# Gated recurrence and gated feed-forward on one core: the first 512 tokens share tiles, banks and copies; weight loads are issued first; the last tile is done in two strips

## The chip, the cores and the metric

The kernel runs on one core of one Trainium2 chip. The metric is the device time of one execution in microseconds. Lower is better.

## The reference

Two layers follow each other over 23,296 tokens (4 sequences of 5,824) with 256 channels. The first is a gated linear recurrence; the second is a feed-forward layer whose two up projections are multiplied.

```python
sig_r, sig_i = sigmoid(r_gate), sigmoid(i_gate)
a_t  = exp(8.0 * sig_r * log(clip(sigmoid(a_param), 1e-6, 1 - 1e-6)))
norm = sqrt(maximum(1 - a_t * a_t, 1e-6))
h[t] = a_t[t] * h[t-1] + norm[t] * sig_i[t] * x[t]       # per channel, h = 0 at the start of each sequence
out  = ((h @ w1) * (h @ w2)) @ w3 @ w_out                # 256 -> 1024, 1024 -> 1024, 1024 -> 256
```

## The kernel before

The tokens are cut into 47 chunks: `sizes = [256, 256] + [512] * 44 + [256]`. Chunks 0 and 1 share the gate stage (they are loaded and gated as one block of 512), but have scans, casts, up products and down products of their own. Channels lie on the 128 partitions in two blocks (`cb`), time along the free axis.

A chunk goes through these steps; the letters are those of the order string, and numbers behind them are the chunk and then a half, channel block or pair:

- `r`, `i`, `x` load the three inputs (SyncE's DMA queue, `load`, L142). `R` and `I` take tanh of half the gate on ScalarE (L150, L162); `p` adds 1 to the second and `t` multiplies it by x (GpSimd, or VectorE where the sets say so; L168, L172).
- `V` and `U` turn both from time-major to channel-major, through TensorE and a PSUM tile for the first chunks (L191), or by a transposing DMA.
- `d` is the exponential that gives a_t (ScalarE, L212), `s` its square, `q` the square root (ScalarE; this and tanh need different tables, and each switch shows as an ACT_TABLE_LOAD), `g` the gated input (VectorE, L237), `h` the scan (VectorE, L251), `y` the cast of the scan's result to bf16 (L268).
- `a` and `b` are the up products with w1 and w2 on TensorE (L286 to L299): 8 blocks of 128 hidden units, in 4 pairs `mp`, each over 2 channel blocks. `c` copies an `a` product from PSUM to SBUF (L307, ScalarE or VectorE), `m` multiplies the copy with the `b` product of the pair (VectorE, L313).
- `D` are the down products of one tile of 128 tokens (8 matmuls that accumulate, L323), `e` copies the sum out of PSUM (L335, L340), `o` stores it.

The product w3 @ w_out is computed once on the chip, into `wp_sb`: `Lw3`, `Cw3` load and cast a block of w3, `Ft` turns it on TensorE, `Fc` copies it out, `Fm` multiplies it with w_out, `Fe` copies the result out with a factor 0.25. `Lw1`, `Lw2`, `Lwo` and `Cw1`, `Cw2`, `Cwo` load and cast the other weights in halves; their fp32 staging tiles are slots of the rings `a` and `nrm`. `A0` to `A3` compute the recurrence's rates from a_param. `W` are groups of two warm-up matmuls on an identity, with no use of the result.

There is no loop over chunks: `ORDER`, a string of some 2,450 steps, says in which order the steps are given out, and each engine runs its own in that order. An instruction that waits holds up all that stand behind it on its engine; DMA issues stand in SyncE's order. Sets such as `DV_COPY`, `AC_SQUARE`, `W_ACT`, `FOLD_ACT` say which engine a step runs on. Tiles come from rings (`RINGS`): PSUM has a ring `po` of 4 banks, for `a` products, down products, turned tiles and the fold, and a ring `pb` of 2 pairs of banks, for `b` products and warm-ups. A step that takes a slot waits until the last user of that slot is done.

The order begins like this:

```python
r0 i0 x0 A3. E A0. A1. A2. R0.1 R0.0 W7 W10 V0.1 V0.0 W3 W14 W4 d0.1 s0.1 d0.0 s0.0 I0 q0.0 t0.0 t0.1 U0 g0
h0.0 W1 W2 W12 W5 W13 W8 W0 W15 h0.1 q0.1 g1 h1.1 h1.0 Lw1.0 Cw1.0 y0.1 y0.0 i2 Lw2.0 I2 r2 Lw1.1 Cw2.0 a0.0.1
a0.0.0 a0.1.0 a0.1.1 b0.0 R2 Cw1.1 x2 y1.1 y1.0 p2 t2.0 Lw3.2 Cw3.2 Lw2.1 Lwo.1 t2.1 c0.0.1 c0.1.1 c0.0.0
```

Of the kernel before, what the change touches and what calls it, by code (L numbers as in the profile page):

```python
# [18 lines left out]
LOG1P = (2.00000001, 0.66666316, 0.40024854, 0.27961419, 0.28174657)  # L19
# [3 lines left out]
def kernel(  # L23
# [59 lines left out]
    DV_PLUS = {16}  # L83
    DV_HALF = set()
    DV_SQUARE = {(0, 1), (11, 0)}
    AC_SQUARE = {(2, 0), (2, 1), (3, 0), (3, 1), (4, 0), (4, 1), (5, 0), (7, 0), (8, 0), (10, 0), (11, 1), (12, 0),
        (14, 0), (14, 1), (15, 0), (15, 1)}
    DV_CAST = set()
    AC_CAST = set()
    DV_COPY = {(0, 0, 0), (0, 0, 1), (0, 1, 0), (0, 1, 1), (0, 2, 0), (1, 0, 0), (1, 0, 1), (1, 1, 0), (1, 1, 1), (1,  # L90
        3, 0), (2, 0, 1), (2, 1, 0), (2, 1, 1), (2, 2, 0), (2, 3, 0), (2, 3, 1), (3, 0, 0), (3, 1, 0), (3, 2, 1), (3,
        3, 0), (4, 0, 0), (4, 0, 1), (4, 1, 1), (4, 2, 0), (4, 2, 1), (5, 1, 1), (5, 3, 0), (5, 3, 1), (6, 0, 0), (6,
        0, 1), (6, 2, 0), (6, 3, 1), (7, 0, 0), (7, 2, 0), (7, 3, 0), (7, 3, 1), (8, 3, 0), (10, 0, 1), (10, 1, 0),
        (10, 1, 1)}
    DV_EVAC = {(2, 0), (8, 0), (8, 1), (9, 0), (9, 1)}
    FOLD_ACT = {('c', 7), ('e', 3), ('e', 4)}
    W_ACT = {('w1', 1), ('w2', 0), ('w3', 0)}
    W_DVE = set()
# [3 lines left out]
    WARM = [2] * 16  # L102
    RINGS = {"r": 4, "i": 5, "x": 4, "th_r": 3, "u": 2, "rt": 2, "ut": 6, "a": 6, "nrm": 6, "h": 2, "y": 4,
# [38 lines left out]
    def load(c, nm):  # L142
        n = width(c) // P
        t = ring(loads, [P, 4, D], F32, name=nm + "_t", tag=nm)
        nc.sync.dma_start(
            out=t[:, :n, :],
            in_=src[nm][starts[c]:starts[c] + width(c), :].rearrange("(p n) c -> p n c" if long_rows(c) else "(n p) c -> p n c", p=P))
        T[nm, c] = t
# [102 lines left out]
    def scan(c, cb):  # L251
        w = sizes[c]
        first = ("h", c) not in T
        if first:
            T["h", c] = ring(ypool, [P, NCB, CT], F32, name="h_t", tag="h")
        h = T["h", c][:, :, :w]
        a, n = (T[key, gates_of(c)][:, :, part(c)] for key in "an")
        if first:
            for b in range(1, B):
                if 0 < b * S - starts[c] < w:  # L260
                    nc.vector.memset(a[:, :, b * S - starts[c]:b * S - starts[c] + 1], 0.0)
        init = 0.0
        if starts[c] % S != 0:
            pw = sizes[c - 1]
            init = T["h", c - 1][:, cb, pw - 1:pw]
        nc.vector.tensor_tensor_scan(h[:, cb, :], a[:, cb, :], n[:, cb, :], init, ALU.mult, ALU.add)  # L266

    def cast(c, cb=None):  # L268
        w = sizes[c]
        if ("y", c) not in T:  # L270
            T["y", c] = ring(ypool, [P, NCB, CT], BF16, name="y_t", tag="y")
        key = c if cb is None else (c, cb)
        cbs = slice(None) if cb is None else cb
        y, h = T["y", c][:, cbs, :w], T["h", c][:, cbs, :w]
# [11 lines left out]
    def up(c, m, dst, w_sb):  # L286
        w = sizes[c]
        for cb in range(NCB):
            nc.tensor.matmul(out=dst[:, :w], lhsT=w_sb[:, cb, m * P:(m + 1) * P],  # L289
                             rhs=T["y", c][:, cb, :w], start=(cb == 0), stop=(cb == NCB - 1))  # L290

    def up_a(c, mp, q):
        T["pa", c, mp, q] = pp = ring(psum_o, [P, CT], F32, name="pa", tag="po")
        up(c, 2 * mp + q, pp, w1_sb)

    def up_b(c, mp):
        T["pb", c, mp] = pp = ring(psum_b, [P, 2, CT], F32, name="pb", tag="pb")
        for q in range(2):
            up(c, 2 * mp + q, pp[:, q, :], w2_sb)  # L299
# [7 lines left out]
    def copy(c, mp, q):  # L307
        w = sizes[c]
        if ("sa", c, mp) not in T:
            T["sa", c, mp] = ring(ffn, [P, 2, CT], BF16, name="sa", tag="sa")  # L310
        copy_to((c, mp, q) in DV_COPY, T["sa", c, mp][:, q, :w], T["pa", c, mp, q][:, :w])

    def product(c, mp):  # L313
        w = sizes[c]
        if ("g", c) not in T:
            T["g", c] = ring(ffn, [P, KD, CT], BF16, name="g_t", tag="g")
        nc.vector.tensor_mul(out=T["g", c][:, 2 * mp:2 * mp + 2, :w], in0=T["sa", c, mp][:, :, :w],  # L317
                             in1=T["pb", c, mp][:, :, :w])

    def pair(c, j2):  # L320
        return min(2, sizes[c] // P - 2 * j2)

    def down(c, j):  # L323
        if c == NCH - 1:
            T["po_last", j] = po = ring(psum_o, [P, D], F32, name="po", tag="po")
        else:
            if ("po", c, j // 2) not in T:
                T["po", c, j // 2] = ring(psum_o, [P, 2, D], F32, name="po", tag="po")
            po = T["po", c, j // 2][:, j % 2, :]
        for k in range(KD):  # L330
            nc.tensor.matmul(out=po,  # L331
                             lhsT=T["g", c][:, k, j * P:(j + 1) * P], rhs=wp_sb[:, k, :],
                             start=(k == 0), stop=(k == KD - 1), skip_group_check=True)
# [6 lines left out]
    def evac_last(c, j):  # L340
        if ("ot", c, j // 2) not in T:
            T["ot", c, j // 2] = ring(ffn, [P, 2, D], F32, name="ot", tag="ot")
        copy_to(j % 2 == 0, T["ot", c, j // 2][:, j % 2, :], T["po_last", j])

    def store_last(c, j):
        t0 = starts[c] + j * P
        nc.sync.dma_start(out=out[t0:t0 + P, :], in_=T["ot", c, j // 2][:, j % 2, :])
# [41 lines left out]
    def fold_t(mi):  # L389
# [244 lines left out]
```

## Time and profile before

| | |
|---|---|
| median of 3 runs | 511.69 us (511.57 to 511.84) |
| the profiled execution | 511.82 us, of which 510.0 us lie between its first and last instruction (the span) |
| busy in the span | TensorE 502.2 us, ScalarE 463.3, VectorE 429.8, GpSimd 318.2 |
| granted TensorE clock | 1.00 in every stage |
| DMA | 124.06 MB, mean 243 GB/s; 387 to 419 GB/s in most stretches of the first 30 us |
| first up product, first down products | 13.30 us, about 47.9 us |

A row of the profile's timeline gives the start in us, the duration in us, the engine, the line, the operation, the tiles written and read, the shape of the operands and the count of merged instructions; in brackets stands how long the engine was idle before it, and what released it. In this table and in the profile, PE is TensorE, PEld its weight loads, DVE VectorE, ACT ScalarE, POOL GpSimd and SPq the instruction queue of SyncE, which issues the DMAs. A busy TensorE can still be one that runs warm-up work, and matmuls overlap, so a sum of durations is more than their time; the distance from start to start is the better measure.

### The profile page before, as it was taken

The numbers are of one execution on the slowest core, as the hardware profiler recorded it, in microseconds if no ns is written. First come the engines' busy times: TensorE is split into PE (matmuls) and PEld (weight loads), VectorE is DVE, ScalarE is ACT, GpSimd is POOL, SyncE is SP. The second block draws the span as 40 slices with busy tenths as digits, with TensorE's granted clock in tenths as the row PEclk, the third lists the DMA queues.
The fourth block names the chain that finished last, engine by engine and source line by source line (L and its number), as shares of the span: only waits on it lengthen the run. The fifth ranks groups of instructions, "written<-read, shape, count | busy, mean of one in ns | idle before, by whom it ended". The sixth has DMA issues, their size and how long they took to land.

```text
span 510.0 us, 8879 instructions
## 1 busy us (share of the span) xinstructions
PE 502.2 (98%) x3217; PEld 308.2 (60%) x3217; DVE 429.8 (84%) x417; ACT 463.3 (91%) x711; POOL 318.2 (62%) x274
## 2 busy tenths in 40 slices
PE   7999999999999999999999999999999999999997
PEld 3777655665565656556666556565566655656566
DVE  5999999999999789878879799878877797959762
ACT  7999999998999999999999999998998979888543
POOL 3775878557558936965786973956647568580200
PEclk9999999999999999999999999999999999999999
DMA  8999999999989997896999996898786895252313
GB/s 319 407 413 307 379 275 276 304 302 257 309 232 282 303 282 248 191 322 184 256 306 317 262 285 163 233 245 227 206 250 151 231 319 149 91 164 64 66 48 105
DMA packets 177904, 124.06 MB, mean 243 GB/s; under 512 B 87362, under 2 KB 173892, under 8 KB 177860
## 3 DMA queue, kind: packets, MB, share of 16 engines
q1 hardware_dynamic: 177856, 123.50, 85.2%
q8 instruction: 25, 0.41, 0.3%
q14 instruction: 19, 0.16, 0.1%
q10 hardware_dynamic: 4, 0.00, 0.0%
HBM read 78.91 MB, written 23.86 MB: 201 GB/s over the span
## 4 chain that ended last, share of the span: by engine, by line
PE 90%; ACT 4%; DVE 2%; issue 2%; DMA 1%; DVEq 0%; ACTq 0%
PE po L331 30%; PE pb L289 29%; PE pa L289 28%; PE pw L403 1%; ACT sa L305 1%; PE ptr L197 1%; DVE g_t L317 1%; DMA r_t<-in_r_gate_dram 1%; PE ptw L392 1%; DVE sa L303 1%; DVE h_t L266 1%; ACT L165 1%; ACT L235 1%; ACT nrm L235 0%; ACT i_t L165 0%
## 5 line engine op out<-in xcount | busy, mean ns | idle before, releaser
L317 DVE TENSOR_TENSOR g_t<-sa,pb 128x1024 bf16<-128x1024 bf16 (+1 forms) x188 | 218.6, 1180 | 60.6 <-PE pb L289 29.0
L289 PEld LDWEIGHTS <-w_sb 128*128 128x128 bf16 x1504 | 146.5, 98 | 144.0 <-issue 3.4
L305 ACT CAST sa<-pa 128x512 bf16<-128x512 f32 (+1 forms) x336 | 180.9, 588 | 27.7 <-PE pa L289 17.6
L289 PE MATMUL pa<-y_t,w_sb 128*128 128x512 bf16 (+1 forms) x752 | 190.6, 372 | 0.4 <-ACT sa L305 0.2
L289 PE MATMUL pb<-y_t,w_sb 128*128 128x512 bf16 (+1 forms) x752 | 185.2, 372 | 0.6 <-DVE g_t L317 0.6
L331 PE MATMUL po<-wp_sb,g_t 128*128 128x256 bf16 x1456 | 178.0, 273 | 0.0
L331 PEld LDWEIGHTS <-g_t 128*128 128x128 bf16 x1456 | 142.4, 98 | 40.6 <-issue 0.5
L278 POOL CAST y_t<-h_t 128x1024 bf16<-128x1024 f32 (+2 forms) x49 | 52.5, 1074 | 146.0 <-DVE h_t L266 142.2
L189 POOL TENSOR_TENSOR u_t<-i_t,x_t 128x512 bf16<-128x512 f32 (+1 forms) x90 | 122.2, 1374 | 4.1 <-issue 2.0
L266 DVE TENSOR_TENSOR_SCAN h_t<-a_t,h_t,nrm 128x512 f32<-128x512 f32 (+1 forms) x92 | 120.8, 1343 | 1.6
L230 POOL TENSOR_TENSOR nrm<-a_t 128x512 f32<-128x512 f32 x74 | 83.0, 1139 | 12.9 <-ACT a_t L220 10.1
L220 ACT ACTIVATE a_t<-rt,la 128x512 f32<-128x512 bf16 (+1 forms) x82 | 66.0, 823 | 0.0
L305 ACT COPY ot<-po 128x512 f32<-128x512 f32 x86 | 50.5, 591 | 12.0 <-PE po L331 11.8
L248 DVE SCALAR_TENSOR_TENSOR nrm<-nrm,ut 128x1024 f32<-128x1024 f32 (+1 forms) x39 | 53.3, 1368 | 5.8 <-ACT nrm L235 5.8
L170 POOL TENSOR_SCALAR i_t<-i_t 128x1024 f32<-128x1024 f32 (+1 forms) x44 | 52.9, 1204 | 7.9 <-ACT i_t L165 7.9
L165 ACT ACTIVATE i_t<-i_t 128x1024 f32<-128x1024 f32 (+1 forms) x46 | 48.9, 1064 | 0.1
L235 ACT ACTIVATE nrm<-nrm 128x1024 f32<-128x1024 f32 (+1 forms) x47 | 48.3, 1041 | 0.2
L159 ACT ACTIVATE th_r<-r_t 128x1024 bf16<-128x1024 f32 (+1 forms) x41 | 43.5, 1060 | 0.0
L303 DVE CAST sa<-pa 128x512 bf16<-128x512 f32 (+1 forms) x40 | 23.4, 615 | 0.6 <-PE pa L289 0.5
L235 ACT ACT_TABLE_LOAD x17 | 21.8, 1283 | 0.3
L165 ACT ACT_TABLE_LOAD x9 | 11.5, 1283 | 0.2
L283 PE MATMUL warm<-ident 128*128 128x512 bf16 x32 | 10.1, 457 | 0.0
(55 smaller groups left out, 119.3 us busy)
## 6 DMA issues: line engine op xcount, KB each, us to landing
r_t<-in_r_gate_dram SPq DMA_DIRECT2D x45, 512.0 KB, 5.3
i_t<-in_i_gate_dram SPq DMA_DIRECT2D x45, 512.0 KB, 5.6
x_t<-in_x_dram SPq DMA_DIRECT2D x45, 512.0 KB, 5.5
out_dram<-ot SPq DMA_DIRECT2D x90, 256.0 KB, 3.3
wf<-in_moe_w_dram SPq DMA_DIRECT2D x12, 512.0 KB, 10.5
wf<-in_moe_w_out_dram SPq DMA_DIRECT2D x2, 512.0 KB, 10.6
rt<-th_r SPq DMA_TRANSPOSE x41, 4.4
ut<-u_t SPq DMA_TRANSPOSE x39, 4.1
```

The source lines that it names most:

```text
L165: nc.scalar.activation(out=t[:, :n, :], in_=t[:, :n, :], func=AF.Tanh, scale=0.5)
L170: (nc.vector if c in DV_PLUS else nc.gpsimd).tensor_scalar(t, t, 1.0, 1.0, op0=ALU.add, op1=ALU.mult)
L189: (nc.vector if (c, half) in DV_HALF else nc.gpsimd).tensor_mul(out=u, in0=t, in1=xt)
L220: nc.scalar.activation(out=a, in_=pr, func=AF.Exp, scale=la4[:, cb:cb + 1], bias=la4[:, cb:cb + 1])
L230: (nc.vector if (c, cb) in DV_SQUARE else nc.gpsimd).tensor_mul(out=n, in0=a, in1=a)
L235: nc.scalar.activation(out=n, in_=n, func=AF.Sqrt, scale=-1.0, bias=1.0)
L248: nc.vector.scalar_tensor_tensor(out=n, in0=n, scalar=1e-3, in1=T["pu", c][:, :, cols], op0=ALU.max, op1=ALU.mult)
L266: nc.vector.tensor_tensor_scan(h[:, cb, :], a[:, cb, :], n[:, cb, :], init, ALU.mult, ALU.add)
L289: nc.tensor.matmul(out=dst[:, :w], lhsT=w_sb[:, cb, m * P:(m + 1) * P], rhs=T["y", c][:, cb, :w], start=(cb == 0), stop=(cb == NCB - 1))
L305: nc.scalar.copy(out=dst, in_=src_ps)
L317: nc.vector.tensor_mul(out=T["g", c][:, 2 * mp:2 * mp + 2, :w], in0=T["sa", c, mp][:, :, :w], in1=T["pb", c, mp][:, :, :w])
L331: nc.tensor.matmul(out=po, lhsT=T["g", c][:, k, j * P:(j + 1) * P], rhs=wp_sb[:, k, :], start=(k == 0), stop=(k == KD - 1), skip_group_che ...
```

## The change

1. **Chunks 0 and 1.** The tiles h, y and g are shared by both, as the gates already were. For each pair of up products with w1 one PSUM bank holds both blocks ([128, 2, 256]), and one copy of 512 elements takes them out, where there were two banks and two copies of 256. The up products themselves stay 256 wide. Down products, their copies and their stores of these 512 tokens are counted as four tiles of chunk 0.
2. **r0** is loaded in two halves by channel block, each in rows of 512 bytes, in the order in which `R0.1`, `R0.0` read them.
3. **Rates.** `rates` takes ten operations instead of eleven: exp(|z|) replaces exp(-|z|), and one multiplication goes.
4. **Last tile.** Its down products are done in two strips of 128 columns, each with a bank, a copy (the first on VectorE, the second on ScalarE) and a store of its own.
5. **Order and engines.** The first 762 steps of `ORDER` (up to chunk 12's early steps) become 755 others; behind them the order is the same. Weight loads now stand ahead of the rates in the order. The casts of w1 go to VectorE (they were on GpSimd and ScalarE), those of w2's first half and of w3's block 0 to GpSimd (both on ScalarE before), that of w3's block 4 to ScalarE; `y0.0` and `y1.1` go from GpSimd to ScalarE; `p2` and `p6` from GpSimd to VectorE; `Fc2` and `Fc3` from VectorE to ScalarE; some squares and copies change sides. A path that turns w3 by DMA is added and not used (`FOLD_DMA` is empty).

```diff
-    DV_PLUS = {16}
+    DV_PLUS = {2, 6, 16}
-    DV_SQUARE = {(0, 1), (11, 0)}
-    AC_SQUARE = {(2, 0), (2, 1), (3, 0), (3, 1), (4, 0), (4, 1), (5, 0), (7, 0), (8, 0), (10, 0), (11, 1), (12, 0),
-        (14, 0), (14, 1), (15, 0), (15, 1)}
+    DV_SQUARE = {(0, 0), (0, 1)}
+    AC_SQUARE = {(2, 0), (2, 1), (4, 0), (4, 1), (6, 0), (8, 0), (9, 1), (10, 1), (11, 0), (11, 1), (12, 0), (14, 0),
+        (14, 1), (15, 0), (15, 1)}
-    AC_CAST = set()
+    AC_CAST = {(0, 0), (1, 1)}
...
-    DV_EVAC = {(2, 0), (8, 0), (8, 1), (9, 0), (9, 1)}
-    FOLD_ACT = {('c', 7), ('e', 3), ('e', 4)}
-    W_ACT = {('w1', 1), ('w2', 0), ('w3', 0)}
-    W_DVE = set()
+    DV_EVAC = {(0, 0), (0, 1), (4, 1), (9, 0), (9, 1)}
+    FOLD_ACT = {('c', 2), ('c', 3), ('c', 7), ('e', 6), ('e', 7)}
+    W_ACT = {('w3', 4)}
+    W_DVE = {('w1', 0), ('w1', 1)}
...
-    def load(c, nm):
+    def load(c, nm, half=None):
         n = width(c) // P
-        t = ring(loads, [P, 4, D], F32, name=nm + "_t", tag=nm)
-        nc.sync.dma_start(
-            out=t[:, :n, :],
-            in_=src[nm][starts[c]:starts[c] + width(c), :].rearrange("(p n) c -> p n c" if long_rows(c) else "(n p) c -> p n c", p=P))
-        T[nm, c] = t
+        cols = slice(None) if half is None else slice(half * P, half * P + P)
+        if (nm, c) not in T:
+            T[nm, c] = ring(loads, [P, 4, D], F32, name=nm + "_t", tag=nm)
+        rows = src[nm][starts[c]:starts[c] + width(c), :]
+        rows = rows.rearrange("(p n) c -> p n c" if long_rows(c) else "(n p) c -> p n c", p=P)
+        nc.sync.dma_start(out=T[nm, c][:, :n, cols], in_=rows[:, :, cols])
...
+    def in_half(c, mp):
+        return c < 2 and mp < HALVED          # HALVED = 4
+
+    def span(c, mp):
+        return part(c) if in_half(c, mp) else slice(0, width(c))
...
     def up_a(c, mp, q):
+        if in_half(c, mp):
+            if ("pa", c, mp) not in T:
+                T["pa", c, mp] = ring(psum_o, [P, 2, sizes[c]], F32, name="pa", tag="po")
+            up(c, mp, q, T["pa", c, mp][:, q, :], w1_sb)
+            return
         T["pa", c, mp, q] = pp = ring(psum_o, [P, CT], F32, name="pa", tag="po")
...
     def copy(c, mp, q):
...
+        if in_half(c, mp):
+            copy_to((c, mp, q) in DV_COPY, T["sa", c, mp][:, :, :sizes[c]], T["pa", c, mp])
+            return
...
+    def strips(c, j):
+        whole = not (c == NCH - 1 and j == sizes[c] // P - 1)
+        return [slice(0, D)] if whole else [slice(0, P), slice(P, D)]
...
     def rates():
-        nc.vector.tensor_scalar(zd, zz, 2.0, None, op0=ALU.add)
-        nc.vector.reciprocal(zd, zd)
-        nc.vector.tensor_mul(out=zz, in0=zz, in1=zd)
+        nc.vector.tensor_scalar(zd, zz, 1e30, 0.5, op0=ALU.min, op1=ALU.add)
+        nc.vector.reciprocal(zz, zd)
         nc.vector.tensor_mul(out=zd, in0=zz, in1=zz)
...
     ORDER = """
+        r0.1 r0.0 i0 x0 Lw1.0 Lw2.0 r2 i2 Lw3.2 Lw1.1 x2 Lwo.1 Lw2.1 Lwo.0 r3 r4 A3. E A0. A1. A2. R0.1 R0.0 W15 W6
+        V0.1 W1 V0.0 d0.1 I0 s0.1 Cw2.0 t0.0 d0.0 s0.0 q0.0 t0.1 W11 W4 W8 W9 U0 q0.1 R2 Cw1.0 g0 h0.1 g1 h0.0 h1.1
+        h1.0 y0.1 W7 W14 W13 W12 W2 W0 W3 V2 W10 I2 p2 y0.0 a0.1.0 a0.1.1 y1.0 y1.1 d2.0 d2.1 s2.0 s2.1 q2 b0.1 a0.0.1
+        a1.1.0 a0.0.0 W5 a1.1.1 a1.0.1 a1.0.0 c0.1.0 m0.1 Cw1.1 Cw3.2 t2.0 t2.1 Cw2.1 b1.1 b0.0 a1.2.1 a1.2.0 c1.1.0
+        c0.0.0 m1.1 Ft2 a0.2.1 a0.2.0 b1.0 c1.0.0 Fc2 c0.2.0 U2 m0.0 c1.2.0 a0.3.0 a0.3.1 b0.2 m1.0 g2 m0.2 h2.0 h2.1
+        Cwo.1 Cwo.0 c0.3.0 R3 R4 b1.2 Fm2 b1.3 a1.3.1 V3 a1.3.0 V4 Lw3.0 Lw3.5 i3 Lw3.1 x3 Lw3.7 Lw3.4 Lw3.6 r7 Lw3.3
```

The bodies of `down`, `evac_last` and `store_last` loop over `strips(c, j)`; `scan`, `cast`, `up_b` and `product` index the shared tiles by `gates_of(c)` and `part(c)`.

## The prediction

> **What bounds the kernel now.** First the page, part 1 and the chain of part 4:
>
> ```profile
> PE 502.2 (98%) x3217; PEld 308.2 (60%) x3217; DVE 429.8 (84%) x417; ACT 463.3 (91%) x711; POOL 318.2 (62%) x274
> PE 90%; ACT 4%; DVE 2%; issue 2%; DMA 1%; DVEq 0%; ACTq 0%
> ```
>
> TensorE is the bound, but its busy time holds warm-up work and latencies, so I count what it must do. In the chain of waits 16 down products of 256 columns take 1.75 us (109 ns each), 8 up products of 512 columns 1.75 us (216 ns), and 8 transposes start 56 ns apart. The page has 1504 up products (96 of them 256 wide), 1456 down, 64 of the weight fold (256 wide) and 160 transposes: 1408 x 0.216 + (96 + 1456 + 64) x 0.109 + 160 x 0.056 = 489.2 us. The change leaves these counts as they are, except that 8 products at the end become 16 of half the width. So the kernel can only win or lose in the 20.8 us (510.0 - 489.2) in which TensorE does nothing useful. Where they lie, by stages and then by order of time:
>
> ```profile
> 25.00:30.00 5.00, 4.95 (x40) 2.88 (x38) 4.43 (x9) 5.00 (x9) 2.85 (x3) 1.00 1.02 419
> 30.00:100.00 70.00, 70.00 (x512) 45.88 (x510) 68.63 (x81) 69.33 (x96) 51.05 (x48) 1.00 1.11 322
> 119.00:124.00 5.00, 4.42 (x22) 1.95 (x20) 5.00 (x5) 3.65 (x6) 3.50 (x3) 1.00 0.90 219
> 140.00:500.00 360.00, 359.81 (x2228) 217.49 (x2226) 296.78 (x245) 325.81 (x515) 226.11 (x186) 1.00 0.79 216
> ```
>
> The columns are the stage, then busy time (and count) of PE, PEld, DVE, ACT, POOL, the clock, DMA. From 30 us on TensorE is full, with one hole near 122 us. The head, in order of time:
>
> ```profile
> 4.40 1.15 ACT L157 ACTIVATE th_r<-r_t 128x512 bf16<-128x512 f32 x2 [1.33 <-DMA r_t<-in_r_gate_dram]
> 5.72 1.45 ACT L220 ACTIVATE a_t<-ptr,la 128x512 f32<-128x512 bf16 x2 [0.18 <-PE ptr L197]
> 10.11 0.75 DVE L245 SCALAR_TENSOR_TENSOR nrm<-nrm,ptr 128x256 f32<-128x256 f32 x2 [0.67 <-ACT nrm L235]
> 13.30 1.04 PE L289 MATMUL pa<-y_t,w_sb 128*128 128x256 bf16 x8
> 14.04 1.42 DVE L303 CAST sa<-pa 128x256 bf16<-128x256 f32 x4
> 22.55 2.45 DVE L266 TENSOR_TENSOR_SCAN h_t<-a_t,h_t,nrm 128x512 f32<-128x512 f32 x2
> 25.07 1.04 POOL L278 CAST y_t<-h_t 128x1024 bf16<-128x1024 f32 x1 [2.85 <-DVE h_t L266]
> ```
>
> The first up product runs at 13.30; then VectorE, busy without a gap over 0.1 us from 10.1 to 27.1 us, sets the pace until chunk 2's scans end at 25.00 and its cast y2 lets chunk 2's up products start at 26.16. Up to there TensorE has done 64 up, 8 fold products and 56 transposes, 11.0 us: 15.1 of the 20.8 us are lost here. The rest: 0.37 in two gaps (25.0, 28.7), 0.74 at 122 us, about 1.4 in small ones, 3.2 behind the last product. The hole:
>
> ```profile
> 117.23 3.36 POOL L189 TENSOR_TENSOR u_t<-i_t,x_t 128x512 bf16<-128x512 f32 x2
> 119.34 2.33 DVE L266 TENSOR_TENSOR_SCAN h_t<-a_t,h_t,nrm 128x512 f32<-128x512 f32 x1
> 122.83 1.02 PE L289 MATMUL pb<-y_t,w_sb 128*128 128x512 bf16 x4 [0.58 <-DVE g_t L317]
> ```
>
> A scan that takes 1.27 us elsewhere took 2.33 beside a GpSimd product, and the product g behind it freed an up bank late.
>
> **The change part by part**, against the profiled execution (511.82 us, span 510.0; the median of the runs is 0.13 lower).
>
> *r by halves.* In the trace a 4 KB packet holds a DMA engine for 159 to 204 ns, one of 1 KB 47, one of 256 B 18 to 26; r0 came in 4 KB packets, the halves come in pieces of 512 B, which no row has. On a line through the rows 512 B costs 28 ns; a half is 32 per engine, 0.90 us, against 1.33 for the whole. The whole landed at 4.37 (chain: 0.74 for 3.63), so the first half lands at 3.94, the second at 4.84, and every later load 0.45 later (bounds: 0, packets as efficient as large ones, to 1.3, each half as long as the whole). ScalarE runs R0.1, R0.0 and d0.1 in order, so R0.0 ends at 5.45 and d0.1 starts at 5.4, not 5.72. The operation taken out of the rates (0.20 us a step; they end at 5.05, not 5.25) counts nothing while R0.0 covers it, 0.2 without.
>
> *Weight loads issued first.* SyncE keeps eight loads outstanding: its issues start at 5.70, 8.76, 11.26 when the load eight before lands, 1.25 to 1.8 us apart. So i0 lands at 5.7, x0 7.0, w1.0 8.8, i2 10.0, w2.0 11.2, r2 12.5 now; after, 6.15, 7.4, w1.0 9.2, w2.0 10.45, r2 11.7, i2 12.95, x2 16.75. Nothing but loads is passed on that queue.
>
> *ScalarE to the first up product.* d0.1, I0 (6.15 to 7.1), d0.0, table load 1.28, q0.0 from 9.1 (9.43 now), q0.1, table load to 11.5, R2 from 11.7, I2 from 12.95 to 14.0, and only then y0.0, which moved from GpSimd to ScalarE: 14.3. The first up product runs near 14.5, 1.2 later than now, and the first copy at 15.15 instead of 14.04.
>
> *VectorE.* Cw1.0 is new ahead of g0. Nearest row for a cast of 128x1024 fp32 on VectorE: the TENSOR_SCALAR of that shape, 0.927, pitch 0.85 (bounds 0.6, half of the 128x1024 two-operand 1.22, to 1.22). w1.0 lands at 9.2, so g0 goes at 10.15 (10.11 now), and h1.0 ends at 14.15. p2 (0.85, moved here) fills the wait for the first copy. From that copy to the end of h2.1: now 10.96 us. After: four copies of 512 at 0.60 replace ten of 256 at 0.34, -1.0; Fc2 goes to ScalarE, -0.6; Cw1.1 comes, +0.85; small waits go, -0.25: 9.95. End 15.15 + 9.95 = 25.1 against 25.00. Cw2.0 on GpSimd now stands beside the scan h0.1, and Cwo.0 beside h2.0; a scan beside a GpSimd operation took from 1.27 (most) to 2.33, so 0 to 1.05 each; I take 0.1, as most paid nothing. Chunk 2 starts at +0.2 (-0.9 to +1.3).
>
> The Trainium skill (SBUF — State Buffer, "Who interferes with whom") says that a VectorE instruction with two SBUF inputs and a GpSimd one that reads SBUF lock each other out whole, the first to start winning. The scan at 119.34 fits it, having waited out the GpSimd product that ended at 120.59. By the rule Cw2.0 (10.5 to 11.5) holds h0.1 up by 0.8 and Cwo.0 h2.0 by 0.3: chunk 2 at +0.6, and the sum 0.4 higher.
>
> *Banks and ScalarE behind it.* c0 and c1 use 8 bank turns instead of 16. ScalarE loses two weight casts net (-1.9), gains Fc2 (+0.9) and two casts y (+0.6), and reaches the end of R4 at 24.95 (25.20 now). The 0.37 us lost at 25.0 and 28.7 were waits at that edge: -0.37 (to +0.7 if the new order is late there).
>
> *Chunks 3 to 11 in a new order.* Chunk by chunk the sums for ScalarE and VectorE differ by under 2 us from now (DVE: two copies, p6 more, Fc3, one square fewer). The hole at 122 us hangs on one scan meeting one GpSimd product; the steps around it are rewritten, and ScalarE copies keep 0.4 us or more ahead of the banks by these sums: -0.74 (to +0.7: another hole).
>
> *The tail.*
>
> ```profile
> 505.98 0.42 DVE L303 COPY ot<-po 128x256 f32<-128x256 f32 x1 [1.69 <-PE po L331]
> 506.43 1.21 SPq L347 DMA_DIRECT2D out_dram<-ot  x2
> 506.90 0.37 ACT L305 COPY ot<-po 128x256 f32<-128x256 f32 x1 [1.21 <-PE po L331]
> ```
>
> 16 products at 56 ns take the place of 8 at 109: +0.02. The last copy has 128 columns: from 0.37 (256) and 0.59 (512), about 0.27: -0.1. The last store is half: -0.15. The first strip goes on VectorE and its store while the second is computed; SyncE's 0.35 us issue for it ends before the last copy does. Together -0.25 (-0.35 to +0.1).
>
> Sum: +0.2 - 0.37 - 0.74 - 0.25 = -1.16: 510.66 by the profiled execution, 510.5 by the runs.
>
> **The rivals.** *No change within 0.2%* (1.02 us, about what a measurement of this kernel can tell): the hole comes back elsewhere, since VectorE stays full to 140 us and GpSimd works beside it; or the halves cost as much as the whole r0, so that r by halves does not do what it says (d0.1 at 6.2, +0.5). Against it: from 30 to 119 us the same load cost nothing. -1.16 + 0.74 or so: 511.3. *Slower:* y0.0 stands behind I2 on ScalarE, I2 waits for i2, and a0.1, all of chunk 0 and 1, d2 and q2 are queued behind. i2 is the eighth issue; by bytes it lands like r2 now, 12.5, but the ninth issue of now, x2, landed at 15.4. Then all is 2.45 us late: 513.0. It decides from 15.1 on (1.02 + 1.16 past 12.95). For it: VectorE idles there, so nothing absorbs a delay. Against: no more bytes are ahead of i2 than now ahead of r2.
>
> **How the numbers follow.** Faster by over 0.2%: 0.45, the sum itself lying just beyond the bound. Within: 0.31. Slower: 0.24, for i2 and for a new order that starves a bank. Likeliest case alone: 509.0 to 510.7. Low end of the range: chunk 2 at -0.9 with the other gains, 509.0; high: i2's case, 513.0, with a small new hole, 513.2.
>
> **What would show it.** R0.1 before 4.1 and d0.1 near 5.4; i2 landing near 13 with I2 idle before it; first 128x512 copy at 15.1; y2 ending near 26.3; TensorE without idle from there to 140 us; last store's copy 0.27. Wrong if chunk 2's products start before 25.3 or after 27.5, or if a hole over 0.5 us stands between 30 and 140.

## The result, and the profile after

The changed kernel is slower: 515.57 us in the median of 14 executions (513.51 to 517.38), against 511.99 us (511.56 to 515.84) of the kernel before on the same chip. The ratio of the two is 1.0069, with a 95% interval of 1.0053 to 1.0084. The forecast was 510.5 with a range up to 513.2, so both its sign and its range were wrong.

The profiled execution took 514.89 us, with a span of 513.1 (before: 511.82 and 510.0). Part 1 and the chain of the page:

```profile
PE 500.0 (97%) x3171; PEld 308.0 (60%) x3225; DVE 431.4 (84%) x416; ACT 462.4 (90%) x707; POOL 313.5 (61%) x271
PE 69%; DVE 7%; ACT 6%; issue 4%; DMA 1%; SPq 1%; DVEq 0%; ACTq 0%
```

The busy times hardly moved. 54 matmul records are missing from this trace (x3171 beside x3225 weight loads), so PE's busy time is not used as a measure. A better yardstick are VectorE's 188 products g, which both kernels run. Against before they are late by 1.15 us at 22 us, 1.18 at 30, 1.45 at 145 and 3.23 at 157, and then by 3.2 to the last one. The span is 3.1 longer. So the loss has two places: 1.15 us ahead of chunk 2, and 1.78 us between 145 and 157 us. From 30 to 145 us 0.3 is lost, and the tail gives back 0.1.

The windows of the changed kernel that answer to the two troubled ones of before (columns as there):

```profile
25.00:30.00 5.00, 4.79 (x43) 2.95 (x42) 4.96 (x8) 5.00 (x9) 3.78 (x4) 1.00 1.03 421
119.00:124.00 5.00, 4.95 (x35) 3.35 (x35) 4.90 (x5) 4.01 (x7) 0.00 (x0) 1.00 1.05 231
```

The hole at 122 us is gone, as predicted. The head in order of time:

```profile
3.62 0.63 ACT L160 ACTIVATE th_r<-r_t 128x512 bf16<-128x512 f32 x1 [0.61 <-DMA r_t<-in_r_gate_dram]
5.44 0.63 ACT L160 ACTIVATE th_r<-r_t 128x512 bf16<-128x512 f32 x1 [1.19 <-DMA r_t<-in_r_gate_dram]
7.31 1.06 ACT L168 ACTIVATE i_t<-i_t 128x1024 f32<-128x1024 f32 x1 [0.58 <-DMA i_t<-in_i_gate_dram]
10.51 0.69 DVE L416 CAST w_sb<-wf 128x1024 bf16<-128x1024 f32 x1
15.38 0.60 PE L299 MATMUL pa<-y_t,w_sb 128*128 128x256 bf16 x4 [0.33 <-ACT y_t L280]
16.14 0.68 DVE L320 CAST sa<-pa 128x512 bf16<-128x512 f32 x1
23.70 2.45 DVE L270 TENSOR_TENSOR_SCAN h_t<-a_t,h_t,nrm 128x512 f32<-128x512 f32 x2
27.31 1.02 PE L299 MATMUL pa<-y_t,w_sb 128*128 128x512 bf16 x3
```

The first half of r lets ScalarE start at 3.62, but then it waits for the second half and for i0. By the trace the halves landed at 3.59 and 5.41, and i0 at 7.29 (before: whole r0 at 4.37, i0 at 5.68). Every load behind is 1.45 to 1.66 us late where it can be compared (x0 8.60 for 6.94, w1.0 10.19 for 8.74). From the first copy (16.14) to the end of h2.1 (26.16) VectorE takes 10.02 us.

The second loss, in order of time on ScalarE and TensorE:

```profile
148.90 1.06 ACT L162 ACTIVATE th_r<-r_t 128x1024 bf16<-128x1024 f32 x1 [1.67 <-DMA r_t<-in_r_gate_dram]
150.48 0.59 PE L299 MATMUL pa<-y_t,w_sb 128*128 128x512 bf16 x2 [1.10 <-ACT sa L322]
151.46 0.59 PE L299 MATMUL pa<-y_t,w_sb 128*128 128x512 bf16 x2 [0.38 <-ACT sa L322]
```

The tanh R18 waits for its load, the copies behind it on ScalarE are late, and TensorE has no bank. Before, r20 was issued at 126.97 and r18 at 139.45, and r18 landed 4.77 us later. Now both are issued together at 141.3 behind a store that waited 4.4 us, and r18 takes 7.56 us. The issue of r18 before:

```profile
139.45 0.60 SPq L145 DMA_DIRECT2D r_t<-in_r_gate_dram  x1
```

and that of r18 and r20 after:

```profile
141.32 1.40 SPq L151 DMA_DIRECT2D r_t<-in_r_gate_dram  x2
```

The place of r18 in the order is that of before; what stands ahead of it and beside it is new. Two of SyncE's waits at 126 to 145 us, both for stores (4.8 us in total, the longest 4.4):

```profile
SPq L380 <- ACT ot L322: 4.8, 2, 4.4
```

The tail:

```profile
509.62 1.35 SPq L376 DMA_DIRECT2D out_dram<-ot  x3
510.11 0.27 ACT L322 COPY ot<-po 128x128 f32<-128x128 f32 x1 [1.23 <-PE po L357]
```

### The profile page after: what moved, and what is told of

Its sections match the earlier page's. It is cut to its first block, busy times and chain, and to the rows that moved or that the text cites. A ratio compares the mean times of both kernels' runs of the same rounds, so it can differ in the third digit from the quotient of the medians.

```text
span 513.1 us, 8834 instructions
## 1 busy us (share of the span) xinstructions
PE 500.0 (97%) x3171; PEld 308.0 (60%) x3225; DVE 431.4 (84%) x416; ACT 462.4 (90%) x707; POOL 313.5 (61%) x271
## 4 chain that ended last, share of the span: by engine, by line
PE 69%; DVE 7%; ACT 6%; issue 4%; DMA 1%; SPq 1%; DVEq 0%; ACTq 0%
PE po L357 24%; PE pb L299 23%; PE pa L299 22%; DVE g_t L337 3%; ACT sa L322 2%; DVE h_t L270 2%; DMA r_t<-in_r_gate_dram 1%; DVE sa L320 1%; SPq L211 1%; ACT ot L322 1%; ACT nrm L238 1%; ACT i_t L168 1%; ACT a_t L223 1%; DVE nrm L251 0%; ACT th_r L162 0%
## 5 line engine op out<-in xcount | busy, mean ns | idle before, releaser
L322 ACT CAST sa<-pa 128x512 bf16<-128x512 f32 (+1 forms) x331 | 179.1, 591 | 26.5 <-PE pa L299 17.7
L299 PE MATMUL pa<-y_t,w_sb 128*128 128x512 bf16 (+1 forms) x721 | 184.9, 372 | 3.1 <-ACT sa L322 1.8
L299 PE MATMUL pb<-y_t,w_sb 128*128 128x512 bf16 (+1 forms) x729 | 182.3, 372 | 1.9
L357 PE MATMUL po<-wp_sb,g_t 128*128 128x256 bf16 (+1 forms) x1464 | 177.4, 272 | 0.4
L270 DVE TENSOR_TENSOR_SCAN h_t<-a_t,h_t,nrm 128x512 f32<-128x512 f32 (+1 forms) x92 | 119.6, 1331 | 1.6
L233 POOL TENSOR_TENSOR nrm<-a_t 128x512 f32<-128x512 f32 (+1 forms) x75 | 82.2, 1115 | 10.3 <-ACT a_t L223 7.5
L173 POOL TENSOR_SCALAR i_t<-i_t 128x1024 f32<-128x1024 f32 (+1 forms) x42 | 50.1, 1196 | 12.8 <-ACT i_t L168 12.8
L320 DVE CAST sa<-pa 128x512 bf16<-128x512 f32 x37 | 24.7, 684 | 2.1 <-PE pa L299 1.1
L231 ACT ACTIVATE nrm<-a_t 128x512 f32<-128x512 f32 x15 | 9.3, 648 | 0.1
```

The lines of the kernel that those rows point to most:

```text
L233: (nc.vector if (c, cb) in DV_SQUARE else nc.gpsimd).tensor_mul(out=n, in0=a, in1=a)
L299: nc.tensor.matmul(out=dst, lhsT=w_sb[:, cb, m * P:(m + 1) * P], rhs=T["y", gates_of(c)][:, cb, span(c, mp)], start=(cb == 0), stop=(cb == ...
L322: nc.scalar.copy(out=dst, in_=src_ps)
L357: nc.tensor.matmul(out=po, lhsT=T["g", c][:, k, j * P:(j + 1) * P], rhs=wp_sb[:, k, cols], start=(k == 0), stop=(k == KD - 1), skip_group_ ...
```

## The experiments

My theory after the result: two separate places cost the time, the second load that r0 in halves makes and the late place of r18 in SyncE's queue. The main rival was that the head is late for another reason (y0.0 behind I2 on ScalarE, a scan beside a GpSimd cast) and that the DMA engines are the limit at 149 us. All runs in one table. "Clock" counts the executions whose mean granted TensorE clock was under 0.9985; of before it was 10 of the 119 executions measured beside them. A 0 there does not mean that all products ran at full pace, as the section on the clock shows.

| run | median us (n) | ratio to before, 95% | clock |
|---|---|---|---|
| changed kernel | 515.57 (14) | 1.0069 (1.0053 to 1.0084) | 3 of 14 |
| whole_r0 | 513.27 (12) | 1.0018 (0.9999 to 1.0037) | 0 of 12 |
| r18_early | 515.33 (9) | 1.0046 (1.0026 to 1.0066) | 5 of 9 |
| whole_r0_r18_early | 512.57 (12) | 1.0008 (0.9992 to 1.0024) | 0 of 12 |
| both_v6_early | 512.34 (12) | 0.9977 (0.9956 to 0.9999) | 0 of 12 |
| before_r_halves | 514.58 (12) | 1.0045 (1.0030 to 1.0059) | 3 of 12 |
| before_r_row_halves | 513.71 (12) | 1.0024 (1.0012 to 1.0036) | 5 of 12 |
| before_halves_act | 516.23 (5) | 1.0080 (1.0066 to 1.0093) | 0 of 5 |
| after_halves_act | 514.66 (5) | 1.0050 (1.0037 to 1.0064) | 2 of 5 |
| halves_warm_moved | 513.70 (12) | 1.0028 (1.0018 to 1.0038) | 0 of 12 |
| before_less_warm | 514.25 (9) | 1.0029 (1.0016 to 1.0042) | 0 of 9 |
| after_warm_moved | 515.79 (12) | 1.0050 (1.0027 to 1.0073) | 1 of 12 |
| pairs_old_order | 513.01 (12) | 1.0013 (0.9999 to 1.0028) | 1 of 12 |
| pairs_scan_moved | 512.00 (12) | 0.9973 (0.9953 to 0.9993) | 0 of 12 |
| before_scan_moved | 511.63 (12) | 0.9981 (0.9958 to 1.0003) | 2 of 12 |

Medians of before beside these runs lay between 511.69 and 512.34, so medians of different runs are not compared finely. The ratios aren't free of chance either: beside both_v6_early, the two runs with a moved scan and after_warm_moved, 7 of the 35 executions of before had a low clock, beside the other runs 3 of 84.

### The two places

```diff
-        r0.1 r0.0 i0 x0 Lw1.0 ...
+        r0 i0 x0 Lw1.0 ...
```

> The changed kernel with r0 as one load again; nothing else differs. My theory: the two half loads of r0 cost about 1.8 us each where the whole one costs 1.3 beyond its start, so all later loads land 1.45 to 1.66 us late and the head keeps 1.15 us of it up to chunk 2. With the whole r0, i0 lands near 5.7, the first up product runs near 13.9 to 14.2, chunk 2's first up product near 26.1 (27.31 now), and the time falls by 1.0 to 1.3 us against the changed kernel, to about 514.4. Rival: the head is late because y0.0 stands behind I2 on ScalarE and because the scan h0.1 runs beside Cw2.0; then the loads move but chunk 2 starts after 26.9 and the time falls by less than 0.4.

Measured: 2.3 us less than the changed kernel by medians, twice what was expected. The profiled execution was a late one (515.06):

```profile
6.63 3.62 PE L287 MATMUL warm<-ident 128*128 128x512 bf16 x8
16.73 1.72 DVE L416 CAST w_sb<-wf 128x1024 bf16<-128x1024 f32 x1
27.55 0.81 PE L299 MATMUL pa<-y_t,w_sb 128*128 128x512 bf16 x2
```

Its i0 landed at 5.46, but eight warm-up products took 3.62 us (2.49 in the changed kernel) and held U0 back, the cast Cw1.1 beside a GpSimd product took 1.72 us (0.68), and chunk 2 started at 27.55, no earlier than in the changed kernel. So this trace does not show the gain at the head; that is read from the next but one run.

```diff
-        x15 ... x16 o8.1 ... o10.0 V17 U15 ... x17 ... V19 r18 r20 R18
+        x15 ... x16 r18 r20 o8.1 ... o10.0 V17 U15 ... x17 ... V19 R18
```

> The changed kernel with the loads r18 and r20 (chunks 18 and 20, far behind the head) passed on SyncE's queue right behind x16, ahead of the stores o10.0, o10.1 and the transposes between; the other queues are the same. My theory: in the changed kernel r18 is issued at 141.32 behind a store that waited 4.4 us for its tile and behind transposes, lands at 148.88 together with r20, R18 waits 1.67 us on ScalarE, the copies behind it are late, and TensorE loses 1.1 + 0.4 us at 150 to 152. Early, r18 lands before 142, R18 does not wait, no hole over 0.5 us stands between 140 and 160, and the time falls by 1.5 to 1.9 us against the changed kernel, to about 513.8. Rival: the DMA engines are the limit there, and what is moved ahead pushes the transposes back: the hole only moves to ScalarE's a_t activations, and the time falls by less than 0.5.

Measured: the holes at 150 are gone; the largest one from 140 to 160 us is 0.07 us. By medians the time fell by only 0.24 us, since 5 of these 9 executions had a clock of 0.996 or 0.997. The four others have a median of 513.70, against 515.21 for the 11 of the changed kernel with a like clock: 1.5 us less. The rival's "less than 0.5" holds for the raw medians and not for the place.

Both edits together, `r0 i0 x0` and `x16 r18 r20`:

> The changed kernel with both edits: r0 whole and r18, r20 early. My theory: the two losses are separate places, so the gains add: 2.6 to 3.1 us under the changed kernel, about 512.6 by the median of its runs, within 0.2% of the kernel before (between 0.0 and +0.8 us against it). Rival: one of the two is absorbed by the other (an earlier head only waits longer at 149 us): then no more than 2 us under the changed kernel.

Measured: 512.57, 3.0 us under the changed kernel and no longer to be told from the kernel before. The gains add up. In its profiled execution (511.80, span 510.0) i0 landed at 5.49, the first up product ran at 14.09, the first copy at 14.72 and chunk 2's first up product at 25.91, 0.25 earlier than before. So in this execution the head without the second load does what it was built for. It does not do so in each: in whole_r0 above and in both_v6_early below i0 landed as early (5.46, 5.44), the eight warm-up products took 3.62 and 3.55 us instead of 2.53 and Cw1.1 1.72 us instead of 0.69, and chunk 2 started at 27.55 and 27.45. The whole r0 takes away the late load, not every late head. The largest hole left from 30 to 140 us is 0.4 us at 52.8 us:

```profile
52.02 0.81 ACT L223 ACTIVATE a_t<-rt,la 128x512 f32<-128x512 bf16 x1 [0.77 <-DMA rt<-th_r]
```

It is the same kind of wait once more: the transpose V6 stands on SyncE's queue behind the load r9.

```diff
-        r8 V5 i5 r9 V6 c3.2.1
+        r8 V5 i5 V6 r9 c3.2.1
```

> The changed kernel with r0 whole and r18, r20 early (as whole_r0_r18_early), and besides the DMA transpose V6 (rt of chunk 6) passed ahead of the load r9 instead of behind it. In whole_r0_r18_early this transpose was issued at 44.68 behind the loads i5 and r9, landed at 51.99, ScalarE waited 0.77 us for it at 52.02, the copy behind was late and TensorE lost 0.40 us at 52.84 (0.66 and 0.88 in two other runs of this order). My theory: V6 lands about one load (1.3 us) earlier, ScalarE does not wait, the hole at 52.84 goes, and the time is 0.3 to 0.6 us under whole_r0_r18_early, near 512.1. Rival: ScalarE's next wait (for a bank or for the other transposes) comes in its place: less than 0.2 us.

Measured: 512.34, 0.23 under whole_r0_r18_early by medians, less than expected; the hole is gone from the trace. The ratio is 0.9977 and its interval ends just below 1, but the median of before beside it is 512.34 too, and the profiled execution, a late one at the head, has a span of 510.9 us. This version is level with the kernel before; that it beats it is not shown.

### What the halves cost

```diff
-        r0 i0 x0 A3. E ...
+        r0.1 r0.0 i0 x0 A3. E ...
```

> The kernel before with r0 loaded as two channel halves; nothing else differs. My theory: the first half lands near 3.6 and the second near 5.4, i0 and all later loads 1.45 to 1.65 us late; R0.0 ends 0.5 us later than now, the first up product runs 1.2 to 1.6 us later, and since VectorE is full from there to 25 us the whole delay stays: 1.0 to 1.5 us slower than before, about 513.2. The prediction's own pricing (each half 0.90 us, later loads +0.45): 0.0 to 0.5 us slower.

Measured: 2.3 us slower by the ratio, more than both prices. i0 landed at 7.85 and the first up product ran at 16.20, 2.9 us later than before. To see whether the small pieces are to blame, the halves were cut by rows:

```diff
-        cols = slice(None) if half is None else slice(half * P, half * P + P)
-        nc.sync.dma_start(out=T[nm, c][:, :n, cols], in_=rows[:, :, cols])
+        js = slice(None) if half is None else slice(half * n // 2, (half + 1) * n // 2)
+        nc.sync.dma_start(out=T[nm, c][:, :n, :][:, js, :], in_=rows[:, js, :])
```

> The kernel before with r0 loaded in two halves as in before_r_halves, but cut by rows: each half has two of a partition's four rows, so its pieces are 2 KB long instead of 512 B; tanh needs both halves before it can start. It tells apart whether the small pieces or the mere second load makes i0 late (in before_r_halves the halves landed at 3.98 and 4.72 and i0 at 7.85; whole, r0 lands at 4.37 and i0 at 5.68). My theory: the pieces; packets of 2 KB took 84 ns in this case's traces, two of them hardly more than one of 4 KB (159), the loads are issued in 0.4 us each and not in 0.6 to 0.7, i0 lands at 5.6 to 6.2, and the time is 0.0 to 0.6 us above before. Rival: every load costs its own handling whatever its pieces, so two halves delay i0 to 7 or later and the time rises by 1 us or more.

Measured: the rival was right. The halves landed at 3.36 and 4.01, earlier than the whole r0, and i0 nevertheless at 7.27, 3.26 us behind the second half:

```profile
7.29 1.06 ACT L166 ACTIVATE i_t<-i_t 128x1024 f32<-128x1024 f32 x1 [0.41 <-DMA i_t<-in_i_gate_dram]
```

The kernel is 1.2 us slower than before by the ratio, against 2.3 us with the column halves; the intervals touch, so whether the small pieces cost something besides is not decided. The loss is in what the DMA engines move between 4 and 6 us (last two columns: their busy share, GB/s). The kernel before, before_r_halves and before_r_row_halves:

```profile
4.00:6.00 2.00, 1.18 (x9) 0.74 (x9) 1.04 (x7) 1.43 (x3) 0.00 (x0) 1.00 1.04 399
```

```profile
4.00:6.00 2.00, 1.36 (x10) 0.91 (x10) 0.98 (x6) 1.88 (x3) 0.00 (x0) 1.00 0.93 229
```

```profile
4.00:6.00 2.00, 1.50 (x10) 0.90 (x10) 1.06 (x7) 1.72 (x3) 0.00 (x0) 1.00 0.62 217
```

With the same bytes in two loads the engines move 217 to 229 GB/s there instead of 399: by 6.0 us 1.42 MB had arrived in the kernel before, 0.94 and 1.04 MB in the two others. The two cuts do not look alike there. With rows the engines were busy for only 0.62 of the time. With columns they were busy for 0.93 of it, but by the trace's packets sixteen of 4 KB that began between 3.9 and 5.1 us held an engine for 0.5 to 1.3 us each, where 159 ns is common; in the kernel before two did, for 0.36 and 0.43 us. The next run asked whether this goes by SyncE's queue.

```diff
-        nc.sync.dma_start(out=T[nm, c][:, :n, cols], in_=rows[:, :, cols])
+        (nc.scalar if half == 0 else nc.sync).dma_start(out=T[nm, c][:, :n, cols], in_=rows[:, :, cols])
```

> The kernel before with r0 as two channel halves (pieces of 512 B) as in before_r_halves, but the second half is issued by ScalarE (behind la_rows, ahead of its first table load) and not by SyncE. My theory: the price goes by the number of loads on SyncE's queue; in all profiles so far i0 landed at 5.4 to 5.8 where it was the second load of that queue and at 7.3 to 8.6 where it was the third, whatever the bytes ahead of it. Here it is the second: it lands at 5.4 to 6.3 and the time is within 0.6 us of before. Rival: the DMA engines handle so many loads in their order, whichever queue they come from: i0 lands at 7 or later and the time is 1.3 to 2.6 us above before, as in before_r_halves.

The same line in both_v6_early, with `r0.1 r0.0` back in its order:

> The changed kernel with its halves of r0, the second issued by ScalarE, and with r18, r20 and the transpose V6 early as in both_v6_early. My theory: i0 lands as in both_v6_early (5.4) or up to 0.9 later, the time is within 0.6 us of both_v6_early (512.3). Rival: i0 at 7 or later, 1.3 us or more above both_v6_early.

Measured: my theory fell. From 4 to 6 us the engines of before_halves_act did move 387 GB/s, but they served the two queues side by side: the second half landed at 6.59, after i0 (6.42), ScalarE waited 2.02 us for it, and the kernel is 4.1 us slower than before. In after_halves_act i0 landed at 7.88, and the kernel is 2.3 us slower than both_v6_early by medians, 3.7 by the ratios. So the engines can be kept fed by a second queue, but not to the use of what is needed first. Why two loads in front slow the engines down at 4 to 6 us stays open; the trace doesn't show what lies between the queue and the engines.

### The clock

In before_r_halves 16 warm-up products took 5.30 us instead of 3.62, and the first up product stands behind them. The granted clock in r18_early at 12 to 16 us (third column from the end):

```profile
12.00:14.00 2.00, 2.00 (x10) 0.91 (x11) 1.80 (x4) 1.98 (x3) 1.04 (x1) 0.55 1.03 419
14.00:16.00 2.00, 2.00 (x7) 0.78 (x6) 2.00 (x6) 1.99 (x3) 0.40 (x1) 0.60 1.05 416
```

and TensorE's order of time there:

```profile
10.72 0.29 PE L200 MATMUL ptr<-ident,u_t 128*128 128x128 bf16 x2 [1.26 <-DVE u_t L189]
11.92 0.60 PE L200 MATMUL ptr<-ident,u_t 128*128 128x128 bf16 x6 [0.92 <-DVE u_t L189]
12.32 4.82 PE L287 MATMUL warm<-ident 128*128 128x512 bf16 x14
```

Fourteen warm-up products took 4.82 us, against 3.19 in the profiled execution of the changed kernel, where the clock read 1.00. TensorE had been waiting for u0, which waits for i0 and x0. Three runs test it. First, the kernel before without six warm-up products that come ahead of u0:

```diff
-        V0.1 V0.0 W3 W14 W4 d0.1 ...
+        V0.1 V0.0 d0.1 ...
```

> The kernel before without three warm-up steps (W3, W14, W4: six products that nothing uses, at 6.0 to 8.8 us); loads and everything else are as before. My theory: TensorE stands idle from 6.2 to 8.9 us, the granted clock falls below 1.0 somewhere in 8 to 16 us in most executions, the 16 warm-up products ahead of the first up product take 4.5 to 6.5 us instead of 3.62, the first up product runs 0.9 to 2.5 us later, and the time rises by as much, with a wider spread from run to run. Rival: the loads and ScalarE set the head, and products that nothing uses cost and bring nothing: the time is within 0.3 us of before.

```profile
8.84 0.39 PE L197 MATMUL ptr<-ident,u_t 128*128 128x128 bf16 x2 [2.69 <-DVE u_t L186]
10.06 6.02 PE L283 MATMUL warm<-ident 128*128 128x512 bf16 x16
```

Measured: 1.5 us slower by the ratio. Loads and ScalarE are as before, TensorE idles 2.69 us, and the 16 products behind take 6.02 us instead of 3.62; the first up product runs at 15.92. Products that nothing uses are worth 1.5 us. But the granted clock did not fall, as the theory had it. It reads 1.00 throughout, and no execution has a mean under 0.9985:

```profile
12.00:14.00 2.00, 2.00 (x6) 0.70 (x5) 1.96 (x5) 2.00 (x3) 0.94 (x3) 1.00 1.06 417
```

By the trace's single products they nevertheless started 0.43 us apart up to 14.75 us, and 0.22 us apart from 15.05 us on. The kernel before has both paces too, also at 1.00: its six warm-up products at 6.00 us started 0.43 us apart, the sixteen at 9.84 us 0.22. The trace's first entry for the clock stands at 14.92 us here and at 9.16 us in the kernel before; ahead of it the column reads 1.00 whatever the pace. So in the head 1.00 is no proof of full pace, and the pace of the products is the better measure. By it TensorE was at full pace at 9.84 us in the kernel before, and without the six products only at about 15 us.

Second and third, two warm-up steps moved ahead of U0:

```diff
-        t0.1 U0 g0 h0.0 W1 W2 W12 ...
+        t0.1 W1 W2 U0 g0 h0.0 W12 ...
```

> The kernel before with r0 as two halves (as in before_r_halves) and two of the warm-up steps (W1, W2: four products that nothing uses) moved ahead of U0 in TensorE's order, so that TensorE works while it waits for u0. In before_r_halves TensorE stood idle from 8.5 to 10.1 us, its granted clock was 0.50 at 12 to 14 us and 0.73 at 14 to 16, and 16 warm-up products took 5.30 us where they took 3.62 in the kernel before; the first up product stands behind them and ran at 16.20. My theory: about half of the cost of the halves is this clock: with the wait filled the clock stays at 1.0, the remaining 12 warm-up products take about 2.7 us, the first up product runs at 14.6 to 15.0, and the time falls by 1.0 to 1.6 us against before_r_halves, to 513.0 to 513.5. Rival: the delay is that of the loads alone, and the warm-up products only fill it: the first up product stays after 15.8 and the time within 0.5 us of before_r_halves.

Measured: 0.9 us under before_r_halves, just short of the range; the first up product ran at 14.94. In the changed kernel:

```diff
-        W11 W4 W8 W9 U0 ... y0.1 W7 W14 W13 W12 ...
+        W11 W4 W8 W9 W7 W14 U0 ... y0.1 W13 W12 ...
```

> The changed kernel, with its half loads, and two warm-up steps (W7, W14: four products that nothing uses) moved ahead of U0 in TensorE's order, so that TensorE works while it waits for u0. My theory: as in halves_warm_moved, a part of the cost of the half loads is the granted clock, which falls in many executions of the changed kernel because u0 is late (0.55 and 0.60 at 12 to 16 us in the profiled run of r18_early); filled, the clock stays at 1.0 and the median falls by 0.5 to 1.2 us against the changed kernel, to 514.4 to 515.0, with fewer executions above 516.5. Rival: the moved products delay U0 by as much as the clock costs: within 0.3 us of the changed kernel.

Measured: no gain by medians, and not decided by the ratios (1.0050 against 1.0069, the intervals overlap). In the profiled execution the moved products ran at full pace and ended at 8.7 us; TensorE again waited 1.34 and 0.92 us, and the clock still fell to 0.62 and 0.53 at 12 to 16 us. In halves_warm_moved the moved products had run until u0 was there. In these two runs warm-up work helped where it reached up to the end of the wait.

### The pair copies and the scan

The changed code under the order of before, to see what banks and copies by pairs do alone (two of the places that differ from the kernel before):

```diff
-        c0.0.1 c0.1.1 c0.0.0 c0.1.0 m0.0 ... D1.1 D1.0 ... e1.0
+        c0.0.0 c0.1.0 m0.0 ... D0.3 D0.2 ... e0.1
```

> The code of the changed kernel (one bank and one copy for each pair of up products of the first two chunks, shared tiles, the rates in ten operations, the last tile in two strips) under the order and the engine choices of the kernel before, with r0 as one load. Of the first two chunks the copies (0,0), (0,1), (1,0), (1,1) are on VectorE and the other four on ScalarE; of a pair's two copies the later place is kept. My theory: four copies of 512 (0.60 us each) in place of ten of 256 (0.34) take 1.0 us off VectorE's chain ahead of h2.1, chunk 2's first up product runs at 25.2 to 25.7 instead of 26.16, and the last strip brings 0.1: 0.5 to 1.1 us faster than before, 510.9 to 511.4. Rival: a bank is free only when the whole pair is copied, so TensorE and with it VectorE wait for banks: chunk 2 starts after 25.9 and the time is within 0.3 us of before.

```profile
21.71 0.38 PE L296 MATMUL pa<-y_t,w_sb 128*128 128x256 bf16 x2 [1.53 <-ACT sa L319]
```

Measured: the rival. A pair's bank is free only when its one copy is done; that copy stood behind nrm on ScalarE, TensorE waited 1.53 us and the products g were 0.9 us late. So the pair copies need an order of their own. Two edits on top, the copy c1.3 on VectorE and the scan h11.1 later:

```diff
-    DV_COPY = {(0, 0, 0), (0, 1, 0), (1, 0, 0), (1, 1, 0), ...
+    DV_COPY = {(0, 0, 0), (0, 1, 0), (1, 0, 0), (1, 1, 0), (1, 3, 0), ...
-        a10.1.0 h11.1 m9.2 m10.0 h11.0 ...
+        a10.1.0 m9.2 m10.0 h11.1 h11.0 ...
```

> pairs_old_order (the changed code under the order of the kernel before, r0 whole) with two edits: the pair copy c1.3 on VectorE instead of ScalarE, so that its bank is free before ScalarE has left nrm (TensorE lost 1.69 us at 20.0 for it), and the scan h11.1 behind m9.2 and m10.0 as in before_scan_moved. My theory: the bank comes at 20.8 instead of 21.6 and the hole at 20 us shrinks to 0.8 or less, chunk 2 starts near 26.2 as in the kernel before, the hole at 122 is gone: 1.3 to 1.8 us under pairs_old_order, 0.5 to 0.9 us faster than before. Rival: the bank's wait moves to the next copy on ScalarE (c0.2, c1.2 behind nrm and a table load): chunk 2 stays 0.9 us late and only the scan's 0.7 us are gained.

Measured: the wait at 20 us fell from 1.69 to 0.83 us and chunk 2 started at 26.28. By the ratio the kernel is faster than before (0.9973); the medians are 512.00 and 512.34, and the profiled execution is 0.5 us longer in span than that of before (it loses 0.9 us anew between 153 and 156 us). So a gain is likely, but the trace does not show it. The scan alone, in the kernel before:

```diff
-        a10.1.0 h11.1 m9.2 m10.0 h11.0 ...
+        a10.1.0 m9.2 m10.0 h11.1 h11.0 ...
```

> The kernel before with the scan h11.1 moved two places back on VectorE, behind the products m9.2 and m10.0 that stood behind it; nothing else differs. In the kernel before this scan took 2.33 us beside a GpSimd product, m9.2 started at 121.59 and TensorE lost 0.74 us at 122. My theory: m9.2 starts at 119.4, the scan starts when the GpSimd product has ended (120.6) and takes 1.27, the hole goes, nobody waits for the scan: 0.6 to 0.8 us faster than before. Rival: the order from 122 to 140 us is as tight as a bank, so the delay comes back at one of the small holes at 129 and 136 us: less than 0.3 us.

```profile
129.39 1.02 PE L289 MATMUL pb<-y_t,w_sb 128*128 128x512 bf16 x4 [0.47 <-DVE g_t L317]
```

Measured: the hole at 122 is gone, and 0.63 us of it came back at 128.5, again behind a product g. The products stand 0.2 us earlier at 145 us. The trace is on the rival's side: most of what the hole gave came back at the next product g. The runs leave it open: the medians are 511.63 and 512.34, and the ratio's interval holds 1.

## Why the prediction was wrong, point by point

- **Later loads +0.45: the term that failed most.** The packets were right (27 ns for 512 B; 28 estimated), and the first half landed at 3.59 (3.94). But the second landed at 5.41 (4.84), d0.1 started at 5.97 (5.4), and i0 landed at 7.29 (6.15). The term counted bytes, and the price lies in the second load: i0 came 1.6 late, by the row cut as well, where the pieces are large. It also missed the issue of a half, 0.61 to 0.68 us instead of 0.39.
- **The steps from i0 to chunk 2** held in one traced execution of three with the whole r0. With the +0.45 taken out they give the first up product at 14.05, the first copy at 14.70 and chunk 2 at -0.25; whole_r0_r18_early measured 14.09, 14.72 and -0.25. In the other two (whole_r0, both_v6_early) chunk 2 was 1.4 and 1.3 us late with an early i0; that eight warm-up products ahead of u0 may take 3.6 us instead of 2.5 was in no term, so the agreement is in part luck. In the changed kernel VectorE's chain was 10.02 for 9.95 predicted, Cw1.0 0.69 for 0.85. The "slower" rival by i2 and y0.0 did not happen: in the changed kernel I2 ran right behind R2, at 13.98.
- **The scan beside Cw2.0:** h0.1 took 1.05 us instead of 0.68, so 0.37, between my 0.1 and the 0.8 that the Trainium skill's rule (SBUF — State Buffer, "Who interferes with whom") gave for the times predicted. The two overlapped for 0.51 us, which by the rule would have cost about that much. The scan h2.0 beside Cwo.0 paid nothing, as Cwo.0 ended at 23.53 before it. In whole_r0_r18_early h0.1 took 0.69.
- **-0.37 for the gaps at 25 and 28.7:** measured about 0. The edge did come earlier: R4 ended at 24.77 in whole_r0_r18_early, for 24.95 predicted (the three terms named there add up to -0.4, not to the -0.25 used). But the products stand at -0.25 at 22 us and -0.23 at 30.
- **-0.74 for the hole at 122:** the hole went, but others came with the new order (in whole_r0_r18_early 0.1 to 0.4 us each at 53, 60, 67, 101 and 111 to 115 us), so from 30 to 145 us 0.3 was lost. The text reasoned from the sums of each engine; they cannot show such meetings.
- **"Nothing but loads is passed on that queue"** was looked at for the weight loads only. Behind chunk 12 the order is the same but for one load: r20 now stands behind r18. That SyncE's queue was the place to look was not seen; the bound "to +0.7: another hole" was too small, and the test "a hole between 30 and 140" stopped 9 us short of the place. Neither of the text's two signs of being wrong showed (chunk 2 started at 27.31, the limit was 27.5), though its sum was 4.2 us off. Which counts for r18, the wait ahead of it or r20 beside it, is open, as the runs moved both.
- **The tail, -0.25:** measured -0.1. The last copy took 0.27 as predicted, but the first strip's store issue (0.42 us, to 510.48) ended after the last copy (510.38), where the text had it end before. From the start of the last copy to its store's landing it is 2.05 us, for 2.11 before.
- **The clock** was no term at all. The trace of before shows 16 warm-up products in 3.62 us; what these would take if u0 is late was not asked, and nor was the pace of the eight that the new order puts ahead of u0.

The sum corrected by the profiled execution: +1.15 (head) +0.3 +1.78 -0.1 = +3.1. The median difference is 3.6; the rest fits the executions at a lower clock (3 of 14, median 517.3, the others 515.21), but was not separated further.

## What to carry to other kernels

Do not price a split load by its bytes alone: here a second load in front of the first critical one cost 1.6 us with pieces of either size. Check in a run what the engines move; a half that lands earlier is worth nothing if what follows it lands later. When an order changes, compare each queue's sequence of transfers too, SyncE's above all, to the end and not only where the text of the change points. Products that nothing uses may carry TensorE's pace: before moving or delaying what TensorE waits for, find what stands between it and the next idle stretch, and read the pace from the products and not from a column alone. One profiled execution is one of several heads: compare its time with the others before a step is called confirmed.

## What the runs showed of the hardware that was not expected

- Two loads of 256 KB in front instead of one of 512 KB: in the profiles of six kernels the DMA engines moved 155 to 261 GB/s from 4 to 6 us, where those with the whole r0 moved 393 to 424, and i0 landed 1.6 to 2.9 us later than in the kernel before, with pieces of 512 B and of 2 KB alike. With the pieces of 512 B the engines' busy share was 0.91 or more all the same.
- A piece of 512 B held an engine for 27 ns, one of 4 KB for 159: 16 x 512 B / 27 ns is 303 GB/s, and 16 x 4096 B / 159 ns is 412. The Trainium skill (DMA: Bandwidth & Descriptors, "Specifications") names 512 B and more as the size for line rate; here that size ran at three quarters of the rate of 4 KB pieces.
- Products of 512 columns started either 0.43 or 0.22 us apart in the head. The slow pace stood ahead of the trace's first entry for the clock, where the column reads 1.00 (up to 14.75 us in before_less_warm), and after waits.
- In r18_early TensorE's clock fell to 0.55 after waits of only 1.26 and 0.92 us with 0.29 us of work between them. The Trainium skill (TensorE: Matmul & The Clock Gate, "Part 1: The HAM clock gate") tells of a free-running window of 3.4 us and of idle gaps longer than that; these waits were shorter. Only 5 of the 9 executions of r18_early had a low clock; that would agree with a window that runs free, but the waits of the other four were not traced.
- Loads on ScalarE's and SyncE's queues are served side by side: a half load issued at 1.32 landed at 6.59, one issued on SyncE's queue at 1.47 to 1.48 at 4.66 to 5.61.
